# Sliding-window attention into a gated FFN on one core: the attention's second product turned round

## The chip, the cores and the metric

The kernel runs on one core of one Trainium2 chip, in a single launch. The metric is device time in microseconds (us). Before the change three runs took 256.97, 258.34 and 258.73 us, a median of 258.34.

## What is computed

Eight batches of eight heads, 576 positions, head dimension 64. Each position attends to itself and the 63 positions before it; the attention output, heads side by side, is the input of an FFN whose two first products are multiplied element by element.

```python
scores = scale * np.matmul(q, k.transpose(0, 1, 3, 2))
rel = pos[:, None] - pos[None, :]
mask = (rel >= 0) & (rel < window)          # window = 64
attn = softmax(np.where(mask, scores, -1e9))
x = np.matmul(attn, v)                      # 4608 rows of 512 after the heads are put side by side
h = (x @ w1) * (x @ w2) @ w3
out = h @ w_out
```

## The kernel before, in words

All matmul inputs are fp16, and sums are fp32. At the start w3 and w_out are multiplied into one 1024x512 matrix `wc_sb` (`fold_t`, `fold_mm`), so that the FFN's second half is one product.

The attention works in 18 stages of 256 rows (four groups of 64 queries, all eight heads). A stage has these steps:

- `scores(s)` (L265): 64 small matmuls give the scores transposed, 128 keys by 64 queries, in two PSUM tiles `a_ps`. The pool `ps_a` has two such buffers, and scores and values take them in turn, so either step waits until the other's results have been read.
- `weigh(d)` (L281), twice a stage: one exponential on ScalarE (ACT) over 128x1024 writes `pt` in fp16, and the band mask is applied, on VectorE (DVE) by a product with `band`, or on GpSimd (POOL) by the two affine selects of `select`. There is no maximum: a constant shift is used.
- `values(s)` (L295): V is the stationary operand and `pt` moves. Per half of the heads, four matmuls with 32 columns of ones (L301) give each query's sum in 32 rows, and 32 matmuls (L307) give the weighted V, already transposed as the FFN needs it (head dimension on the partitions, queries along the row).
- `norm(s)` (L311): ACT takes Ln of the sums and Exp of minus that, which gives the reciprocals `r`; DVE multiplies both halves by them into `xT` (L320), a ring of 2048 rows.
- `keep_sums(s)` (L324) sends the logarithms by a DMA of the SP queue to `lnsum`. `check_sums` (L451) tests them near the end; if any is out of bounds a general path, which is not taken here, runs behind the fast one.

The FFN works in nine groups of 512 rows. `ffn_ab(g, fc)` (L355) makes eight matmuls of 512 columns, an ACT copy and a DVE product; there are eight of these in a group. `ffn_o(g, t)` (L374), four in a group, makes eight matmuls and one copy out of PSUM, on DVE or ACT. The pool `ps_f` has four buffers, two for each `ffn_ab`.

Inputs arrive by DMAs of the POOL queue. q and k are transposed in 32x32 blocks on DVE (`transposes`, L214). `RUN` says how many rows of q or k lie next to each other in a load: nine for the first three batches, two after that. The transposed words are written with a step of that many words. `copy_v` (L232) copies V rows by half a block, on DVE.

The order of the work is written out by hand (`manual_schedule`): each engine works through its own list in the order in which the program calls the steps. Up to stage 5 every call stands in the program by itself (L479 to L642). From then on a loop takes an FFN slot, then the attention's steps that are due (`tick`, L336): each stage has six units, scores and the first `weigh` at unit 0, the second at unit 1, `values` and `norm` of the stage before at unit 3, `keep_sums` at unit 5. `events` (L328) sets at which unit, counted from a batch's first, its loads, transposes and copies of V are issued.

Of the kernel before, what the change touches and what calls it, by code (L numbers as in the profile page):

```python
# [15 lines left out]
P = 128  # L16
# [123 lines left out]
def kernel(  # L140
# [25 lines left out]
    NU = 6 * NS + 6  # L166
    AHEAD = 18
    START = 42

# [54 lines left out]
    def load_v(b, *blocks):  # L224

        vh = v16s[b % 3]
        for c in blocks:
            lo = D if c == 7 else 0
            s0 = 64 * c + lo
            nc.gpsimd.dma_start(out=vh[lo:P, c], in_=v[b, :, s0:s0 + P - lo, :].rearrange("h s d -> s h d"))  # L230

    def copy_v(b, half, i0, i1):  # L232

        vh = v16s[b % 3].rearrange("p (i o) h d -> p i o (h d)", o=2)
        if half == 0:
            dve_cp(vh[0:D, i0:i1, 1], vh[D:P, i0:i1, 0])
        else:
            dve_cp(vh[D:P, i0:i1, 1], vh[0:D, i0 + 1:i1 + 1, 0])
# [13 lines left out]
    def make_band():  # L252

        nc.gpsimd.memset(band, 1.0)
        select(band)
        nc.gpsimd.memset(band[:, 4], 1.0)
        nc.gpsimd.affine_select(out=band[:, 4], in_=band[:, 4], pattern=[[1, 64]], compare_op=ALU.is_ge,
                                fill=0.0, base=0, channel_multiplier=-1)
# [22 lines left out]
    def weigh(d, engine=nc.gpsimd):  # L281

        pt = probs[d] = sb.tile([P, 4, W], FP16, name="pt", bufs=6)
        nc.scalar.activation(pt, held.pop(d).rearrange("k j (a n) -> k (j a) n", a=2), AF.Exp, bias=-SHIFT, scale=scale)  # L284
        first = [i for i, (b, t) in enumerate(groups(d // 2)) if t == 0]
# [9 lines left out]
    def values(s):  # L295

        o_ps = opened[s] = [ps_a.tile([P, 2, 512], FP32, name="a_ps") for _ in range(2)]
        for jp in range(2):
            pt = probs.pop(2 * s + jp)
            for h in range(4):  # L300
                nc.tensor.matmul(o_ps[0][32 * h:32 * h + 32, 1, W * jp:W * jp + W], ones32, pt[:, h],  # L301
                                 start=True, stop=True, skip_group_check=True)
            for i, (b, t) in enumerate(groups(s)):
                for x in range(2):
                    for h in range(4):
                        o0 = W * x + 64 * i
                        nc.tensor.matmul(o_ps[jp][32 * h:32 * h + 32, 0, o0:o0 + 64],  # L307
                                         v16s[b % 3][:, max(0, t - 1), 4 * jp + h, x:D:2], pt[:, h, 64 * i:64 * i + 64],
                                         start=True, stop=True, skip_group_check=True)

    def norm(s):  # L311

        o_ps = opened.pop(s)
        y = lns[s] = sb.tile([P, 2, W], FP32, name="ln_s", bufs=3)
        r = sb.tile([P, 2, W], FP32, name="r")
        x0 = s * W % RING
        nc.scalar.activation(y, o_ps[0][:, 1].rearrange("p (j n) -> p j n", j=2), AF.Ln)  # L317
        nc.scalar.activation(r, y, AF.Exp, scale=-1.0)  # L318
        for jp in range(2):
            nc.vector.tensor_tensor(xT[:, 2 * jp:2 * jp + 2, x0:x0 + W],  # L320
                                    o_ps[jp][:, 0].rearrange("p (x n) -> p x n", x=2),
                                    r[:, jp].unsqueeze(1).broadcast_to([P, 2, W]), ALU.mult)

    def keep_sums(s):  # L324
        nc.sync.dma_start(out=lnsum[4 * s:4 * s + 4, :], in_=lns.pop(s)[0:P:32].rearrange("a j n -> a (j n)"))
# [120 lines left out]

    rows = 4 * NS
    okv = const.tile([rows, 1], FP32)
    ones = const.tile([rows, 1], FP32)

    def check_sums():  # L451

        chk = const.tile([rows, 2 * W], FP32)
        nc.gpsimd.memset(ones, 1.0)
        nc.gpsimd.tensor_tensor(chk, lnsum, lnsum, ALU.mult)
        nc.gpsimd.tensor_single_scalar(chk, chk, BOUND * BOUND, op=ALU.is_le)
        nc.vector.tensor_reduce(okv, chk, axis=mybir.AxisListType.X, op=ALU.min)
        nc.vector.tensor_scalar(okv, okv, -1.0, 1.0, op0=ALU.mult, op1=ALU.add)
# [15 lines left out]
    def make_ones(engine):  # L474
        engine.memset(ones32, 1.0)

# [56 lines left out]
    values(0)  # L533
    norm(0)
    fold_mm(5, 0, DM, dve_cp)
# [5 lines left out]
    values(1)  # L541
    norm(1)
    fold_mm(6, 0, DM, dve_cp)
# [5 lines left out]
    ffn_ab(0, 2)  # L549
    keep_sums(0)  # L550
    ffn_ab(0, 3)
# [22 lines left out]
    load_v(2, 6, 7)  # L574
    keep_sums(1)
    store()
    norm(2)
    transposes(2, 'k', 0)
# [3 lines left out]
    store()  # L582
    norm(3)
    transposes(2, 'k', 1)
# [9 lines left out]
    store()  # L594
    keep_sums(2)
    scores(4)
# [3 lines left out]
    weigh(9, nc.gpsimd)  # L600
    keep_sums(3)
    weigh(8, nc.gpsimd)
# [16 lines left out]
    values(4)  # L619
    norm(4)  # L620
    transposes(3, 'k', 1)
# [5 lines left out]
    store()  # L627
    norm(5)
    keep_sums(4)
    ffn_o(1, 1, act_cp)  # L630
# [8 lines left out]
    load_qk(4, 'k')  # L639
    keep_sums(5)  # L640
    store()
# [14 lines left out]
    for i, (w, due) in enumerate(slots):  # L656
# [9 lines left out]
        while u < NU and u + 1 <= due + 1e-6:  # L666
# [5 lines left out]

    bad = nc.values_load(bad_i[0:1, 0:1], min_val=0, max_val=4 * NS,
                         skip_runtime_bounds_check_because="a count of 72 flags")
    with tc.If(bad > 0, preferred_fallthrough_block=True, label="range"):
# [30 lines left out]
```

## Time and profile before

| | before |
|---|---|
| runs | 256.97, 258.34, 258.73 us |
| profiled execution, first to last instruction (span) | 256.9 us |
| TensorE (PE) clock granted | 0.999 |
| PE busy | 242.7 us (94%) |
| DVE busy | 146.1 us (57%) |
| ACT busy | 117.9 us (46%) |
| POOL busy | 114.2 us (44%) |

The profiled execution has no time of its own beside its span of 256.9 us: that span is 1.4 us under the median of the runs and next to the fastest of them. Matmuls are pipelined, so that busy time counts several in flight at once; the chain of work that ended last, followed back from the last instruction, says what each stretch of PE work costs in the end. In a row of the chain the first number is the start, the second the time, and "x4" the instructions in it. In a row of the timeline the second number is the time from the first start to the last end.

### The profile page before, as it was taken

The page shows a single profiled execution, that of the slowest core. Times are in us where ns is not written, and L with a number is a line of the kernel's source. Part 1 is how long each engine was busy: PE and PEld are TensorE (multiplying, and loading weights), DVE is VectorE, ACT ScalarE, POOL GpSimd, SP SyncE. Part 2 cuts the span into 40 slices and gives each one's busy share as a digit, 9 for nine tenths or more (in the row PEclk, how much of TensorE's full clock was granted, in tenths as well). Part 3 has the DMA queues.
Part 4 walks back from the last instruction along what each step waited for, and adds up shares of the span by engine and source line. Part 5 has one row for each costly group of instructions (what it writes and reads, how often), then busy time and mean ns, then how long its engine had stood idle before and what let it go on. Part 6 is the DMA issues. An engine that isn't in the chain of part 4 may idle for free.

```text
span 256.9 us, 8221 instructions
## 1 busy us (share of the span) xinstructions
PE 242.7 (94%) x3592; PEld 127.1 (49%) x3592; DVE 146.1 (57%) x218; ACT 117.9 (46%) x177; POOL 114.2 (44%) x153
## 2 busy tenths in 40 slices
PE   2959999999999999999999999999999999999990
PEld 2948654454454544445444444544444445444450
DVE  0346956869676546557764774775566345425330
ACT  3033643385565754454526444545465355233310
POOL 7973857759599746890197036003000303003000
PEclk9999999999999999999999999999999999999999
DMA  6999999979997999699089909501300220031022
GB/s 199 196 202 183 205 205 194 168 143 165 193 142 88 191 197 141 99 192 177 2 124 207 118 0 156 105 5 41 126 3 5 82 87 4 0 126 43 4 82 88
DMA packets 75657, 30.09 MB, mean 117 GB/s; under 512 B 62488, under 2 KB 70040, under 8 KB 75616
## 3 DMA queue, kind: packets, MB, share of 16 engines
q0 software_dynamic: 69712, 18.88, 73.6%
q1 hardware_dynamic: 5616, 10.44, 11.1%
q8 instruction: 29, 0.48, 0.8%
q10 hardware_dynamic: 288, 0.20, 0.2%
q14 instruction: 12, 0.10, 0.1%
HBM read 38.80 MB, written 9.44 MB: 188 GB/s over the span
## 4 chain that ended last, share of the span: by engine, by line
PE 90%; DMA 6%; ACT 1%; issue 1%; DVE 0%; POOLq 0%
PE f_ps L367 49%; PE f_ps L383 24%; PE f_ps L444 6%; PE a_ps L275 4%; PE a_ps L307 4%; DMA ab<-in_moe_w_out_dram 4%; PE a_ps L301 2%; DMA q<-in_q_dram 2%; PE f_ps L437 1%; ACT pt L284 1%; DVE w3T L439 0%; DVE t2k L390 0%; ACT t2k L390 0%; PE f_ps L462 0%; POOLq L701 0%
## 5 line engine op out<-in xcount | busy, mean ns | idle before, releaser
L367 PE MATMUL f_ps<-xT,w_sb 128*128 128x512 f16 x576 | 129.4, 379 | 0.0
L367 PEld LDWEIGHTS <-w_sb 128*128 128x128 f16 x576 | 54.7, 98 | 64.3 <-issue 0.4
L371 DVE TENSOR_TENSOR ab<-f_ps,a_sb 128x512 f16<-128x512 f32 x72 | 49.6, 689 | 40.5 <-PE f_ps L367 38.1
L383 PE MATMUL f_ps<-wc_sb,ab 128*128 128x512 f16 (+1 forms) x296 | 65.6, 374 | 0.0
L370 ACT COPY a_sb<-f_ps 128x512 f32<-128x512 f32 x72 | 42.2, 587 | 47.2 <-PE f_ps L367 47.2
L245 POOL TENSOR_SCALAR_AFFINE_SELECT pt<-pt 128x1024 f16<-128x1024 f16 x11 | 12.6, 1143 | 79.7 <-ACT pt L284 79.6
L383 PEld LDWEIGHTS <-ab 128*128 128x128 f16 x296 | 27.9, 98 | 31.0
L284 ACT ACTIVATE pt<-a_ps 128x1024 f16<-128x1024 f32 x36 | 36.2, 1027 | 12.4 <-PE a_ps L275 12.3
L320 DVE TENSOR_TENSOR xT<-a_ps,r 128x512 f16<-128x512 f32 x36 | 23.2, 686 | 23.5 <-ACT r L318 23.4
L230 POOL DMA_DIRECT2D v<-in_v_dram x40 | 33.8, 862 | 2.3 <-DMA w_sb<-in_moe_w_dram 1.2
L386 ACT COPY t2k<-f_ps 128x512 f32<-128x512 f32 (+1 forms) x21 | 12.1, 576 | 43.4 <-PE f_ps L383 43.4
L288 DVE TENSOR_TENSOR pt<-pt,band 128x1024 f16<-128x1024 f16 x25 | 17.3, 696 | 15.4 <-ACT pt L284 15.2
L210 POOL DMA_DIRECT2D k<-in_k_dram x32 | 20.2, 645 | 6.7 <-DMA v<-in_v_dram 3.3
L210 POOL DMA_DIRECT2D q<-in_q_dram x32 | 20.4, 652 | 4.9 <-DMA v<-in_v_dram 1.9
L220 DVE STREAM_TRANSPOSE qT<-q 128x576 int32<-128x576 int32 x16 | 14.7, 930 | 8.2 <-DMA q<-in_q_dram 8.2
L444 PE MATMUL f_ps<-ab,w3T 128*128 128x256 f16 (+1 forms) x96 | 14.8, 308 | 3.4 <-DMA ab<-in_moe_w_out_dram 3.0
L220 DVE STREAM_TRANSPOSE kT<-k 128x576 int32<-128x576 int32 x16 | 14.8, 936 | 1.1 <-DMA k<-in_k_dram 1.1
L307 PE MATMUL a_ps<-pt,v 128*32 128x64 f16 x1152 | 14.2, 193 | 0.3 <-issue 0.3
L317 ACT ACTIVATE ln_s<-a_ps 128x512 f32<-128x512 f32 x18 | 10.7, 597 | 7.6 <-PE a_ps L301 7.4
L386 DVE COPY t2k<-f_ps 128x512 f32<-128x512 f32 x15 | 10.3, 686 | 6.8 <-PE f_ps L383 6.8
L275 PEld LDWEIGHTS <-kT 32*128 32x128 f16 x1152 | 10.4, 92 | 7.3 <-issue 7.2
L307 PEld LDWEIGHTS <-v 128*32 128x32 f16 x1152 | 13.6, 97 | 0.8 <-issue 0.4
(47 smaller groups left out, 129.1 us busy)
## 6 DMA issues: line engine op xcount, KB each, us to landing
out_dram<-t2k SPq DMA_DIRECT2D x35, 256.0 KB, 3.4
q<-in_q_dram POOLq DMA_DIRECT2D x32, 144.0 KB, 6.2
k<-in_k_dram POOLq DMA_DIRECT2D x32, 144.0 KB, 7.1
v<-in_v_dram POOLq DMA_DIRECT2D x32, 128.0 KB, 5.6
w_sb<-in_moe_w_dram POOLq DMA_DIRECT2D x8, 256.0 KB, 9.7
w_sb<-in_moe_w_dram SPq DMA_DIRECT2D x2, 512.0 KB
ab<-in_moe_w_out_dram POOLq DMA_DIRECT2D x2, 512.0 KB, 9.4
xT<-in_moe_w_dram POOLq DMA_DIRECT2D x2, 512.0 KB, 12.2
```

What stands on the lines that cost most here:

```text
L210: nc.gpsimd.dma_start(out=t16_of(b, which)[32 * j:32 * j + 32].rearrange("p hh (i n) -> p (hh i) n", n=r * D), in_=src[b, 2 * j:2 * j + 2] ...
L220: nc.vector.transpose(dst[b][:, hh].rearrange("q t c -> q (t c)").bitcast(I32).rearrange("q (i p r) -> q i r p", p=32, r=r), t16s[which, b ...
L230: nc.gpsimd.dma_start(out=vh[lo:P, c], in_=v[b, :, s0:s0 + P - lo, :].rearrange("h s d -> s h d"))
L284: nc.scalar.activation(pt, held.pop(d).rearrange("k j (a n) -> k (j a) n", a=2), AF.Exp, bias=-SHIFT, scale=scale)
L307: nc.tensor.matmul(o_ps[jp][32 * h:32 * h + 32, 0, o0:o0 + 64], v16s[b % 3][:, max(0, t - 1), 4 * jp + h, x:D:2], pt[:, h, 64 * i:64 * i + ...
L320: nc.vector.tensor_tensor(xT[:, 2 * jp:2 * jp + 2, x0:x0 + W], o_ps[jp][:, 0].rearrange("p (x n) -> p x n", x=2), r[:, jp].unsqueeze(1).br ...
L367: nc.tensor.matmul(d[:, f * n:f * n + n], w[:, dc, (fc + f) * P:(fc + f + 1) * P], xT[:, dc, x0:x0 + n], start=(dc == 0), stop=(dc == 3), ...
L370: act_cp(a_sb[:, 0:nf * n], a_ps[:, 0:nf * n])
L371: nc.vector.tensor_tensor(ab[:, fc:fc + nf, lo:hi], b_ps[:, 0:nf * n].rearrange("p (f n) -> p f n", f=nf), a_sb[:, 0:nf * n].rearrange("p ...
L383: nc.tensor.matmul(o_ps[:, 0:c1 - c0], ab[:, fc, t * P:t * P + P], wc_sb[:, fc, c0:c1], start=(fc == 0), stop=(fc == 7))
L386: cp(o_sb[:, c0:c1], o_ps[:, 0:c1 - c0])
L444: nc.tensor.matmul(o_ps[:, c0:c1], w3Ts[fc][:, ec, :], wo16[:, ec, c0:c1], start=(ec == 0), stop=(ec == 7))
```

## The change

- The stationary operand of the second product is now `pt`: 32 queries at a time, every second one of a group of 64 (`c` is 0 for the even and 1 for the odd queries). V moves, with a 65th column of ones, so that each query's sum comes out as column 64 of its own row. The ones matmuls go. The V tiles have rows of 96 elements per head (`VW`) to hold the ones.
- The exponential reads every second query of the scores, so that `pt` holds the even queries of a group, then the odd ones; the masks have the same order.
- `norm(s, jp)` works on one half of the heads: a DVE reciprocal of 128x8 sums, a DVE product of 128x512 into `xn`, and a DVE 32x32 block transpose of 128x256 words (pairs of fp16) into `xT`. Ln and Exp go. The first half is issued right after `values`, the second one unit later.
- `keep_sums` and its 18 DMAs go; the reciprocals stay in `rs`, and `check_sums` tests them with three operations on POOL of 128x288.
- In the loop all copies of `ffn_o` go to ACT (even t had been on DVE); the transposes and the second `copy_v` are issued at other units.
- In the part written out by hand, `norm(s, 0)` and `norm(s, 1)` stand where `norm(s)` stood.

```diff
-    lnsum = const.tile([4 * NS, 2 * W], FP32)
-    ones32 = const.tile([P, 32], FP16)
-    v16s = [const.tile([P, 8, H, D], FP16, name=f"v16_{i}") for i in range(3)]
+    rs = const.tile([P, NS, 2, 8], FP32)
+    v16s = [const.tile([P, 8, H, VW], FP16, name=f"v16_{i}") for i in range(3)]
...
     def select(rows):
-        pat = [[0, rows.shape[1]], [1, 64]]
+        pat = [[0, rows.shape[1]], [1, 2], [2, 32]]
+        rows = rows.rearrange("p m (c i) -> p m c i", c=2)
...
-        nc.scalar.activation(pt, held.pop(d).rearrange("k j (a n) -> k (j a) n", a=2), AF.Exp, bias=-SHIFT, scale=scale)
+        nc.scalar.activation(pt.rearrange("k h (g c i) -> k (h g) c i", g=4, c=2),
+                             held.pop(d).rearrange("k j (g i c) -> k (j g) c i", c=2, i=32), AF.Exp, bias=-SHIFT, scale=scale)
...
-            for h in range(4):
-                nc.tensor.matmul(o_ps[0][32 * h:32 * h + 32, 1, W * jp:W * jp + W], ones32, pt[:, h],
-                                 start=True, stop=True, skip_group_check=True)
             for i, (b, t) in enumerate(groups(s)):
-                for x in range(2):
+                for c in range(2):
                     for h in range(4):
-                        o0 = W * x + 64 * i
-                        nc.tensor.matmul(o_ps[jp][32 * h:32 * h + 32, 0, o0:o0 + 64],
-                                         v16s[b % 3][:, max(0, t - 1), 4 * jp + h, x:D:2], pt[:, h, 64 * i:64 * i + 64],
+                        n0 = 64 * i + 32 * c
+                        o0 = 256 * (i % 2) + 128 * c
+                        nc.tensor.matmul(o_ps[jp][32 * h:32 * h + 32, i // 2, o0:o0 + D + 1], pt[:, h, n0:n0 + 32],
+                                         v16s[b % 3][:, max(0, t - 1), 4 * jp + h, 0:D + 1],
                                          start=True, stop=True, skip_group_check=True)
...
+    def norm(s, jp):
+        o = opened[s][jp].rearrange("p k (g c n) -> p (k g) c n", g=2, c=2)
         x0 = s * W % RING
-        nc.scalar.activation(y, o_ps[0][:, 1].rearrange("p (j n) -> p j n", j=2), AF.Ln)
-        nc.scalar.activation(r, y, AF.Exp, scale=-1.0)
-        for jp in range(2):
-            nc.vector.tensor_tensor(xT[:, 2 * jp:2 * jp + 2, x0:x0 + W],
-                                    o_ps[jp][:, 0].rearrange("p (x n) -> p x n", x=2),
-                                    r[:, jp].unsqueeze(1).broadcast_to([P, 2, W]), ALU.mult)
+        r = rs[:, s, jp].rearrange("p (g c) -> p g c", c=2)
+        xn = sb.tile([P, 4, D, 2], FP16, name="xn", bufs=4)
+        nc.vector.reciprocal(r, o[:, :, :, D])
+        nc.vector.tensor_tensor(xn.rearrange("p g d c -> p g c d"), o[:, :, :, 0:D],
+                                r.unsqueeze(3).broadcast_to([P, 4, 2, D]), ALU.mult)
+        nc.vector.transpose(
+            xT[:, 2 * jp:2 * jp + 2, x0:x0 + W].bitcast(I32).rearrange("p x (g i) -> p x g i", i=32),
+            xn.rearrange("p g d c -> p (g d c)").bitcast(I32).rearrange("p (g e x) -> p x g e", e=32, x=2))
...
+        k0, k1, q0, q1 = (-10, -7, -5, -4) if b > 4 else (-7, -5, -4, -1)
-                       (-7, (transposes, "k", 0)), (-5, (transposes, "k", 1)), (-4, (transposes, "q", 0)),
-                       (-2, (transposes, "q", 1)), (2, (copy_v, 0, 0, 4)), (4, (copy_v, 1, 0, 3))):
+                       (k0, (transposes, "k", 0)), (k1, (transposes, "k", 1)), (q0, (transposes, "q", 0)),
+                       (q1, (transposes, "q", 1)), (2, (copy_v, 0, 0, 4)), (5, (copy_v, 1, 0, 3))):
...
             values(s - 1)
-            norm(s - 1)
-        if m == 5 and START // 6 <= s <= NS:
-            keep_sums(s - 1)
+            norm(s - 1, 0)
+        if m == 4 and START // 6 <= s <= NS:
+            norm(s - 1, 1)
...
     def make_ones(engine):
-        engine.memset(ones32, 1.0)
+        for vh in v16s:
+            engine.memset(vh[:, :, :, D:D + 2], 1.0)
...
-        part += [lambda g=g, t=t: ffn_o(g, t, act_cp if t % 2 else dve_cp) for t in range(4)]
+        part += [lambda g=g, t=t: ffn_o(g, t, act_cp) for t in range(4)]
```

More of the change, by code (lines that the diff above doesn't have):

```diff
@@ L1 @@
+import math
 from contextlib import ExitStack
@@ L167 @@
     AHEAD = 18
+    VW = 96
     START = 42
@@ L445, in fold_mm @@
         cp(wc_sb[:, fc, c0:c1], o_ps[:, c0:c1])
-    rows = 4 * NS
-    okv = const.tile([rows, 1], FP32)
-    ones = const.tile([rows, 1], FP32)
+    okv = const.tile([P, 1], FP32)
+    ones = const.tile([P, 1], FP32)
     def check_sums():
-        chk = const.tile([rows, 2 * W], FP32)
+        sums = rs.rearrange("p s j n -> p (s j n)")
+        chk = [const.tile([P, 16 * NS], FP32, name=f"chk_{i}") for i in range(2)]
         nc.gpsimd.memset(ones, 1.0)
-        nc.gpsimd.tensor_tensor(chk, lnsum, lnsum, ALU.mult)
-        nc.gpsimd.tensor_single_scalar(chk, chk, BOUND * BOUND, op=ALU.is_le)
-        nc.vector.tensor_reduce(okv, chk, axis=mybir.AxisListType.X, op=ALU.min)
+        nc.gpsimd.tensor_single_scalar(chk[0], sums, math.exp(-BOUND), op=ALU.is_ge)
+        nc.gpsimd.tensor_single_scalar(chk[1], sums, math.exp(BOUND), op=ALU.is_le)
+        nc.gpsimd.tensor_tensor(chk[0], chk[0], chk[1], ALU.mult)
+        nc.vector.tensor_reduce(okv, chk[0], axis=mybir.AxisListType.X, op=ALU.min)
         nc.vector.tensor_scalar(okv, okv, -1.0, 1.0, op0=ALU.mult, op1=ALU.add)
@@ L533 @@
     values(0)
-    norm(0)
+    norm(0, 0)
+    norm(0, 1)
     fold_mm(5, 0, DM, dve_cp)
@@ L541 @@
     values(1)
-    norm(1)
+    norm(1, 0)
+    norm(1, 1)
     fold_mm(6, 0, DM, dve_cp)
@@ L574 @@
     load_v(2, 6, 7)
-    keep_sums(1)
     store()
-    norm(2)
+    norm(2, 0)
+    norm(2, 1)
     transposes(2, 'k', 0)
@@ L582 @@
     store()
-    norm(3)
+    norm(3, 0)
+    norm(3, 1)
     transposes(2, 'k', 1)
@@ L594 @@
     store()
-    keep_sums(2)
     scores(4)
@@ L619 @@
     values(4)
-    norm(4)
+    norm(4, 0)
+    norm(4, 1)
     transposes(3, 'k', 1)
@@ L627 @@
     store()
-    norm(5)
-    keep_sums(4)
+    norm(5, 0)
+    norm(5, 1)
     ffn_o(1, 1, act_cp)
@@ L671 @@
     fast.close()
-    bad = nc.values_load(bad_i[0:1, 0:1], min_val=0, max_val=4 * NS,
-                         skip_runtime_bounds_check_because="a count of 72 flags")
+    bad = nc.values_load(bad_i[0:1, 0:1], min_val=0, max_val=P,
+                         skip_runtime_bounds_check_because="a count of 128 flags")
     with tc.If(bad > 0, preferred_fallthrough_block=True, label="range"):
```

20 lines of the change are left out of this document (6 added, 14 removed).

## The prediction

> **What bounds the kernel now.** I read the page first: its span, the busy times, and the chain of work that ended last.
>
> ```profile
> span 256.9 us, 8221 instructions
> ...
> PE 242.7 (94%) x3592; PEld 127.1 (49%) x3592; DVE 146.1 (57%) x218; ACT 117.9 (46%) x177; POOL 114.2 (44%) x153
> ...
> PE 90%; DMA 6%; ACT 1%; issue 1%; DVE 0%; POOLq 0%
> ```
>
> TensorE (PE) is 90% of the chain. ScalarE (ACT) and VectorE (DVE) are almost absent from it, so work taken off ACT is worth nothing by itself, and work given to DVE costs nothing until DVE makes PE wait. Next, the same chain in order of time, one values step of the loop:
>
> ```profile
> 106.35 0.22 PE a_ps L301 x4
> 106.58 0.24 PE a_ps L307 x32
> 106.82 0.11 PE a_ps L301 x4
> 106.93 0.24 PE a_ps L307 x32
> 107.18 3.56 PE f_ps L383 x16
> 110.73 1.73 PE f_ps L367 x8
> ```
>
> The step takes 107.18 - 106.35 = 0.83 us. The second four ones matmuls take 0.11, the first four 0.22: the other 0.11 is paid at the entry from the wide matmuls, whoever comes first. One FFN slot of eight matmuls is 1.73, so one wide matmul is 0.216. Then the groups by line, which price what goes and what comes:
>
> ```profile
> L284 ACT ACTIVATE pt<-a_ps 128x1024 f16<-128x1024 f32 x36 | 36.2, 1027 | 12.4 <-PE a_ps L275 12.3
> ...
> L320 DVE TENSOR_TENSOR xT<-a_ps,r 128x512 f16<-128x512 f32 x36 | 23.2, 686 | 23.5 <-ACT r L318 23.4
> ...
> L318 ACT ACTIVATE r<-ln_s 128x512 f32<-128x512 f32 x18 | 11.3, 630 | 0.6
> L317 ACT ACTIVATE ln_s<-a_ps 128x512 f32<-128x512 f32 x18 | 10.7, 597 | 7.6 <-PE a_ps L301 7.4
> ...
> L463 DVE CAST bad_i<-f_ps 1x1 int32<-1x1 f32 x1 | 0.1, 136 | 0.0
> ```
>
> Last, DVE's load by stretch, since an average of 57% hides where it is full (the columns are PE, PEld, DVE, ACT, POOL):
>
> ```profile
> 24.00:38.00 14.00, 14.00 (x293) 8.71 (x291) 10.91 (x19) 7.41 (x10) 9.37 (x14) 1.00 1.32 202
> ...
> 50.00:66.00 16.00, 15.91 (x329) 7.89 (x328) 13.24 (x18) 9.70 (x15) 12.16 (x15) 1.00 1.17 166
> ...
> 90.00:114.00 24.00, 23.67 (x367) 11.60 (x366) 13.22 (x20) 11.50 (x18) 17.57 (x23) 1.00 1.40 152
> ```
>
> DVE is 10.91 of 14 us busy around stages 0 and 1, and 13.24 of 16 around stages 2 and 3, against 13.22 of 24 in the loop. The prediction turns on the first two.
>
> **The change, part by part.** PE first. Without the ones matmuls a values step is 0.11 (entry) + 0.24 + 0.24 = about 0.60, with 1/64 of the 0.48 more for the 65th column. Weights stay 128x32, and 32 matmuls follow each other as before. Saving 0.22 a stage, 18 x 0.22 = 4.0 us if nothing else happens.
>
> ACT loses 18 x (0.60 + 0.63) = 22 us and gains 14 `ffn_o` copies; it is not on the path. The exponential of 1.03 us now reads every second element; no row shows that. I take it as unchanged and put its price under the rivals.
>
> DVE loses two products a stage and gains two halves of `norm`. Two rows price an instruction that waits for the one before it on DVE, and two the block transposes:
>
> ```profile
> 58.69 1.22 DVE L220 STREAM_TRANSPOSE kT<-k 128x576 int32<-128x576 int32 x1
> ...
> 73.90 0.78 DVE L220 STREAM_TRANSPOSE qT<-q 128x576 int32<-128x576 int32 x1
> ...
> 79.65 1.43 DVE L220 STREAM_TRANSPOSE kT<-k 128x576 int32<-128x576 int32 x2
> ```
> ```profile
> 234.97 0.68 DVE L457 TENSOR_REDUCE okv<-chk 72x1 f32<-72x512 f32 x1 [0.59 <-POOL chk L456]
> 235.69 0.15 DVE L458 TENSOR_SCALAR okv<-okv 72x1 f32<-72x1 f32 x1
> ```
>
> The second instruction reads the first's result and starts 235.69 - 234.97 - 0.68 = 0.04 after its end. Independent ones start before the last has ended: two transposes take 1.43, so the second starts 1.43 - 0.78 = 0.65 after the first, 0.13 before its end. The new transpose has 256 words, not 576: in proportion 0.29, with a fixed part of 0.1 to 0.15 about 0.33 until the next may start (estimate from these rows). The reciprocal of eight numbers out of PSUM I put at 0.16, just above the 0.136 of the one-element cast. So one half of `norm` holds DVE for 0.16 + 0.04 + 0.69 + 0.04 + 0.33 = 1.26 us. From below 1.2 (0.14 and 0.29); from above 1.6, if the transpose pays for its stepped reading what the transpose at 58.69 pays for writing with a step of nine words where the others have two (1.22 against 0.78 for 576 words: 0.76 ns a word, 0.2 in all) and the reciprocal twice its price. I take 1.26, as a step of two words is what the 0.78 row has.
>
> The Trainium skill, "VectorE: DVE Perf Modes", section "Walkthrough: the 8-slice pipeline in each mode", says that the reciprocal runs its divide with a repeat count of eight. At its 0.96 GHz that would be an estimated 0.07 for eight numbers instead of 0.01, a half of 1.32 and a sum 0.6 us higher; no run here shows it.
>
> Now PE, ACT and DVE are followed through the part written by hand, in the clock of before. **Stages 0 and 1:**
>
> ```profile
> 30.90 1.29 DVE L320 TENSOR_TENSOR xT<-a_ps,r 128x512 f16<-128x512 f32 x2
> 32.11 0.68 DVE L445 CAST wc_sb<-f_ps 128x512 f16<-128x512 f32 x1
> 32.80 0.29 DVE L236 COPY v<-v 64x512 f16<-64x512 f16 x1
> 33.01 0.68 DVE L439 COPY w3T<-f_ps 128x1024 f16<-128x1024 f16 x1
> ```
> ```profile
> 28.67 0.22 PE a_ps L301 x4
> ...
> 31.32 0.89 PE f_ps L437 x16
> ...
> 33.04 3.56 PE f_ps L444 x16
> 36.60 13.81 PE f_ps L367 x64
> ```
>
> DVE gets to `norm(0)` at 30.90 both before and after, since work queued ahead of it ends then. After: first product done 31.79, second at 30.90 + 1.26 + 0.16 + 0.04 + 0.69 = 33.05, DVE free at 33.42. `values(1)` could start at 32.0 (31.32 + 0.89 less 0.22), but its second half needs the buffer that the second product frees: 33.10, so it ends at 33.35 and the two `fold_mm` behind it at 36.91. DVE goes on with the cast (0.69), the copy (0.21) and w3T (0.61): `norm(1)` starts at 34.93 and ends, last transpose in full, at 37.56. The first `ffn_ab` starts at 36.91, has two matmuls' worth of `xT`, waits until 37.61 and ends at 37.61 + 6 x 0.216 = 38.91. Before: 36.60 + 1.73 = 38.33. **+0.58.**
>
> **Stages 2 and 3:**
>
> ```profile
> 56.50 0.68 DVE L386 COPY t2k<-f_ps 128x512 f32<-128x512 f32 x1
> ```
> ```profile
> 56.40 1.83 PE f_ps L383 x8
> ...
> 59.24 1.83 PE f_ps L383 x8
> 61.08 0.47 PE f_ps L367 x2
> ...
> 61.55 4.91 PE f_ps L367 x22
> ```
>
> Before, `ffn_ab(1, 0)` started at 61.08, did the two matmuls that the first product had made ready, and went on at 61.55: nothing was to spare. After: DVE starts `norm(2)` at 57.11 (56.50 + 0.68, less 0.07 of overlap), as it no longer waits for Ln and Exp, and frees the buffers at 58.00 and 59.26. PE ends `ffn_o(0, 2)` at 58.01, `values(3)` gets its second buffer at 59.31 and ends at 59.56, `ffn_o(0, 3)` at 61.39. On DVE the k transpose (1.22 - 0.13 = 1.09 until the next) stands behind `norm(2)` from 59.63, so `norm(3)` starts at 60.72 and ends at 63.35. `ffn_ab(1, 0)` then does its last six matmuls from 63.40, ending at 64.70, against 61.55 + 1.30 = 62.85. **+1.85.** The two transposes and the product behind it are as late as before relative to PE, so no more is lost.
>
> **Stages 4 and 5:** two values steps save 0.44; the second waits 0.1 for `norm(4)`. **-0.35.** **Stages 6 to 17:** `norm` starts about 0.45 after the step's start and ends 2 x 1.26 + 0.1 later, at 3.1; the first wide matmul that needs it comes 0.60 + 3.56 = 4.16 after that start. Slack 1.1, and no DVE copy stands between, since the copies moved to ACT; the moved transposes stand at units with an FFN slot ahead of the step. 12 x 0.22: **-2.64.**
>
> At nothing: `keep_sums` (SP, nobody on the path waits), `check_sums` (three POOL operations, idle POOL, DVE reads them a slot later), the longer selects (POOL waits for ACT most of the time), memsets at the start (DVE waits for q), `copy_v` (runs of 64 stay together; were it paid like the product, 0.69 for 512 elements, the 2048 and 1536 elements copied ahead of stage 2 would take 4.8 us, some 2 of them beyond the slack).
>
> Sum: 0.58 + 1.85 - 0.35 - 2.64 = -0.56, say -0.6. Against the execution's span, 256.9 to 256.3; it stands 1.4 below the runs' median, so in that measure 258.34 - 0.6 = **257.7**. Each 0.1 us more in a half of `norm` delays the first two stretches by four halves each: about 0.8, and with stages 4 and 5 about 1 us.
>
> **The rivals.** *The gain stays:* 18 x 0.22 off, 254.4. For it speaks that DVE idles 43%; against, that 61.08 and 61.55 leave no slack and one product alone, 0.69, is longer than the 0.6 that a half had. *DVE as the bound:* a strided fp16 write slows the product, or the transpose is dear. At the 0.76 ns a word above the product would be 1.08; already at a half of 1.6 the sum is -0.6 + 3.4: 261.1, slower by 1%; that is where it decides. *The exponential pays for its step:* 1024 x 0.76 ns, 1.8 us instead of 1.03. The waits of stage 2 and 3 for two pairs of them grow by 1.6 each and the start by 0.8: +4, 261.7. The loop would hide it, with three slots between scores and values. *PE does not gain:* loads of `pt` are not hidden and each four matmuls take 60 ns, not 30: 288 x 0.03 = 8.6 more, 266. Same shapes speak against it.
>
> The Trainium skill, "PSUM — Partial Sum Buffer", section "Specifications (TRN2)", says that PSUM has lines of 8 bytes and that any access that isn't contiguous slows matmuls significantly; it says that of matmuls, and no run here shows whether ScalarE's reads are meant. By it the exponential's rival would hold.
>
> **How the numbers follow.** Forecast 0.55, gain stays 0.15, DVE as the bound 0.15, exponential 0.10, PE 0.05. About 1%, 2.6 us, is what a measurement tells from no change. The first is within 1% (its own range 257.1 to 259.5, for halves of 1.2 to 1.44); the second is faster; the others slower, but for 0.03 of a milder exponential. Faster 0.15, same 0.58, slower 0.27. The range runs from the second, 254.4, to just short of the exponential in full, 261.6; PE's rival and the dearer half of DVE's stay out.
>
> **What would show it.** Values steps of 0.6 in the chain; exponentials of 1.03; halves of 1.26 on DVE; waits of PE for DVE at `values(1)`, `values(3)` and at the first `ffn_ab` of groups 0 and 1, about 3 us in all, and none in the loop. Wrong if DVE's halves are longer or the loop's first `ffn_ab` waits as well.

## The result, and the profile after

| | before | after |
|---|---|---|
| runs | 256.97 to 258.74 us (4) | 284.09 to 286.28 us (4) |
| median | 258.53 us | 284.70 us |
| after / before | | 1.103 (95%: 1.099 to 1.108) |
| profiled execution: time | none of its own | 284.09 us |
| profiled execution: span | 256.9 us | 282.4 us |

The kernel became slower by 26 us, where 0.6 us less was forecast. A run's time stands 1.7 to 1.9 us above its span in the runs listed here (284.09 against 282.4), so the span of 256.9 of before belongs to a run of about 258.6 us, near the median, and not to the fastest. The page of after, the same three lines as were shown of before:

```profile
span 282.4 us, 7897 instructions
...
PE 242.2 (86%) x3448; PEld 124.5 (44%) x3448; DVE 161.0 (57%) x278; ACT 104.2 (37%) x155; POOL 118.5 (42%) x154
...
PE 66%; DVE 16%; DMA 7%; issue 3%; ACT 3%; POOL 2%; DVEq 0%; POOLq 0%; ACTq 0%
```

PE is busy as long as before (242.2 us against 242.7) in a span that is 25.5 us longer, and DVE has 16% of the chain of work that ended last, where it had 0%. So PE is not busy for longer; it waits for DVE. The view of waits of after says where (in total, how often, the longest):

```profile
PE f_ps L367 <- DVE xT L322: 20.4, 14, 2.0
...
PEld L367 <- DVE xT L322: 3.8, 2, 2.1
...
PEld L437 <- DVE xT L322: 3.3, 1, 3.3
...
PE f_ps L437 <- DVE xT L322: 2.8, 1, 2.8
```

L322 is the new transpose, L367 the wide matmuls of `ffn_ab`, L437 a step of the fold of w3 (`fold_t`). The wide matmuls wait fourteen times, 1.5 us on average, where the prediction had two such waits, at the first slots of groups 0 and 1. Twelve of them, 19.1 us, lie in the loop, two in each of groups 2 to 7. To place them, take four marks of the chain in order of time: the first matmul of group 0 (36.60 before), the last six of `ffn_ab(1, 0)` (61.55), the first of group 2, and the last run of `ffn_o`. Of before:

```profile
86.21 1.73 PE f_ps L367 x8
...
244.17 6.94 PE f_ps L383 x40
```

And of after, with a part of the loop between:

```profile
39.88 13.81 PE f_ps L367 x64
...
67.06 4.91 PE f_ps L367 x22
...
91.76 1.73 PE f_ps L367 x8
...
101.36 0.74 DVE xn L320
102.12 0.46 DVE xT L322
102.62 1.69 PE f_ps L367 x7
104.40 0.69 DVE ab L371
105.09 0.13 DVE rs L319
105.24 0.74 DVE xn L320
106.00 0.46 DVE xT L322
106.50 2.97 PE f_ps L367 x13
...
115.37 0.64 PE a_ps L309 x62
116.00 3.56 PE f_ps L383 x16
119.56 1.73 PE f_ps L367 x8
...
129.28 0.46 DVE xT L322
129.78 1.92 PE f_ps L367 x8
...
133.39 0.46 DVE xT L322
133.89 3.18 PE f_ps L367 x14
...
268.80 6.94 PE f_ps L383 x40
```

After lags by 3.28 at the first mark, 5.51 at the second, 5.55 at the third and 24.63 at the fourth. The loop from group 2 on lasted 157.96 us before and 177.04 after: 19.1 us are lost there, and 0.9 more in the tail behind the fourth mark (12.73 before, 13.60 after). In that loop PE is idle for 19.9 us (177.04 less 157.10 busy), and was idle for 0.3 before. In the chain both halves of an even stage's `norm` stand in PE's way, each followed by the matmuls of an FFN slot less one (x7) or less three (x13 is five and a whole slot); in groups 3 and 7 by a whole slot (x8) or a slot less two (x14 is six and a whole slot). Each half stands on DVE behind the `ab` product of an FFN slot just done (the rows from 104.40 on), and so comes late for the next slot. An odd stage (115.37) costs nothing: `ffn_o`, which does not read `xT`, follows it for 3.56 us.

The matmuls done ahead of the wait, one or three in most groups, are the clue. In the loop a stage writes the columns of `xT` for the *next* group; the slots that wait belong to the *current* one and read other columns. The list of waits in the built program says which matmuls of `ffn_ab` wait for a write of `norm`, past the first matmul of a group (`dc` is the row of `xT` that a matmul reads, `fc` the slot):

```
before          every group but 2           fc 0: dc 2
after           groups 2, 4, 5, 6           fc 0: dc 2    fc 4: dc 1    fc 5: dc 3
after           groups 3, 7 (ring wraps)    fc 0: dc 2    fc 4: dc 0    fc 5: dc 2
```

A transpose writes two stretches, the same 256 columns in rows 2jp and 2jp+1 of the 4x2048 tile. If a wait is derived for everything from the first to the last word written, half 0 at column x0 covers the rest of row 0 and all of row 1 up to x0+256: the current group's columns, left of x0, are in it for `dc` 1. Half 1 hits `dc` 3 in the same way. Where the ring wraps, x0 is 0 and the current group lies at columns 1536 to 2047, inside row 0 and row 2: `dc` 0 and `dc` 2. These are the pairs of the list. The same reading gives the wait at L437: half 1 of stage 0 covers all of row 2, where a piece of w3 is parked. The product that wrote `xT` before had the same two stretches and no such wait; it wrote 16-bit elements, the transpose writes 32-bit words through a view of the 16-bit tile. (Group 2 is missing in the line of before, since an earlier matmul there already waits for that product.)

### The profile page after: what moved, and what is told of

Read it like the earlier page. It is cut to its first block, busy times and chain, and to the rows that moved or that the text cites. A ratio compares the mean times of both kernels' runs of the same rounds, so it can differ in the third digit from the quotient of the medians.

```text
span 282.4 us, 7897 instructions
## 1 busy us (share of the span) xinstructions
PE 242.2 (86%) x3448; PEld 124.5 (44%) x3448; DVE 161.0 (57%) x278; ACT 104.2 (37%) x155; POOL 118.5 (42%) x154
## 4 chain that ended last, share of the span: by engine, by line
PE 66%; DVE 16%; DMA 7%; issue 3%; ACT 3%; POOL 2%; DVEq 0%; POOLq 0%; ACTq 0%
PE f_ps L367 40%; PE f_ps L383 17%; DVE xn L320 5%; PE f_ps L444 4%; PE a_ps L278 4%; DVE ab L371 3%; DMA ab<-in_moe_w_out_dram 3%; DVE xT L322 3%; DMA k<-in_k_dram 2%; ACT pt L287 2%; DMA q<-in_q_dram 2%; PE a_ps L309 2%; POOL v L231 1%; PE f_ps L437 1%; DVE rs L319 1%
## 5 line engine op out<-in xcount | busy, mean ns | idle before, releaser
L367 PE MATMUL f_ps<-xT,w_sb 128*128 128x512 f16 x576 | 131.2, 379 | 21.3 <-DVE xT L322 20.4
L367 PEld LDWEIGHTS <-w_sb 128*128 128x128 f16 x576 | 54.6, 98 | 87.7 <-issue 21.4
L247 POOL TENSOR_SCALAR_AFFINE_SELECT pt<-pt 128x1024 f16<-128x1024 f16 x11 | 14.3, 1302 | 96.8 <-ACT pt L287 96.8
L287 ACT ACTIVATE pt<-a_ps 128x1024 f16<-128x1024 f32 x36 | 36.2, 1026 | 12.4 <-PE a_ps L278 12.3
L386 ACT COPY t2k<-f_ps 128x512 f32<-128x512 f32 (+1 forms) x35 | 20.3, 580 | 48.9 <-PE f_ps L383 48.9
L320 DVE TENSOR_TENSOR xn<-a_ps,rs 128x512 f16<-128x512 f32 x36 | 26.2, 729 | 1.2
L292 DVE TENSOR_TENSOR pt<-pt,band 128x1024 f16<-128x1024 f16 x25 | 17.4, 701 | 12.8 <-ACT pt L287 12.5
L211 POOL DMA_DIRECT2D q<-in_q_dram x32 | 20.4, 649 | 8.0 <-DMA v<-in_v_dram 4.0
L322 DVE STREAM_TRANSPOSE xT<-xn 128x256 int32<-128x256 int32 x36 | 16.0, 445 | 1.2
L249 POOL TENSOR_SCALAR_AFFINE_SELECT pt<-pt 128x1024 f16<-128x1024 f16 x11 | 14.6, 1331 | 0.8
L309 PEld LDWEIGHTS <-pt 128*32 128x32 f16 x1152 | 10.6, 95 | 9.1 <-issue 6.8
L309 PE MATMUL a_ps<-v,pt 128*32 128x65 f16 x1152 | 13.0, 195 | 1.6 <-DVE xn L320 1.3
L319 DVE RECIPROCAL rs<-a_ps 128x8 f32<-128x8 f32 x36 | 6.7, 186 | 13.1 <-PE a_ps L309 13.1
```

The lines of the kernel that those rows point to most:

```text
L211: nc.gpsimd.dma_start(out=t16_of(b, which)[32 * j:32 * j + 32].rearrange("p hh (i n) -> p (hh i) n", n=r * D), in_=src[b, 2 * j:2 * j + 2] ...
L287: nc.scalar.activation(pt.rearrange("k h (g c i) -> k (h g) c i", g=4, c=2), held.pop(d).rearrange("k j (g i c) -> k (j g) c i", c=2, i=32 ...
L309: nc.tensor.matmul(o_ps[jp][32 * h:32 * h + 32, i // 2, o0:o0 + D + 1], pt[:, h, n0:n0 + 32], v16s[b % 3][:, max(0, t - 1), 4 * jp + h, 0: ...
L320: nc.vector.tensor_tensor(xn.rearrange("p g d c -> p g c d"), o[:, :, :, 0:D], r.unsqueeze(3).broadcast_to([P, 4, 2, D]), ALU.mult)
L322: nc.vector.transpose(xT[:, 2 * jp:2 * jp + 2, x0:x0 + W].bitcast(I32).rearrange("p x (g i) -> p x g i", i=32), xn.rearrange("p g d c -> p ...
L367: nc.tensor.matmul(d[:, f * n:f * n + n], w[:, dc, (fc + f) * P:(fc + f + 1) * P], xT[:, dc, x0:x0 + n], start=(dc == 0), stop=(dc == 3), ...
```

## Experiments

The theory: **a false wait.** The framework that builds the program derives, for a write of 32-bit words in two stretches into the 16-bit tile, a wait that spans both; the loss is that wait. The rivals: **DVE is too slow or its order is wrong** (the prediction's own rival, with copies and moved transposes as variants), and **the new instructions themselves cost PE time**.

**e1, one unbroken stretch a write.** `xT` is laid out by stages, so that the two rows of a transpose lie side by side. The pieces of w3 that are parked in `xT` move to the slots of stages 4 to 7; all else stays.

```diff
-    xT = const.tile([P, NJ, RING], FP16)
+    xT = const.tile([P, RING // W, NJ, W], FP16)
...
-            xT[:, 2 * jp:2 * jp + 2, x0:x0 + W].bitcast(I32).rearrange("p x (g i) -> p x g i", i=32),
+            xT[:, x0 // W, 2 * jp:2 * jp + 2, :].bitcast(I32).rearrange("p x (g i) -> p x g i", i=32),
...
-                                     xT[:, dc, x0:x0 + n], start=(dc == 0), stop=(dc == 3), skip_group_check=True)
+                                     xT[:, x0 // W:(x0 + n) // W, dc, :], start=(dc == 0), stop=(dc == 3), skip_group_check=True)
```

> The changed kernel with the ring xT laid out by stages: 8 slots of 4x256 instead of 4 rows of 2048, so that each transpose writes one unbroken stretch; nothing else differs. Theory W (wide wait): the transpose writes 32-bit words into a 16-bit tile in two stretches, and the wait that the framework derives covers everything from the first to the last word, so that TensorE waits for a norm whose rows it does not read. Then the waits of L367 for the transpose (20.4 us) fall below 3 us, the fold's wait (2.8 us) goes, and the span falls from 282.4 to about 259 (257 to 262). Theory D (VectorE is the bound: the longer halves of norm, 1.35 us, are late by themselves): the order on VectorE and its work are the same, so the span stays above 276.

Measured: 261.17 us median (260.54 to 263.31), 1.010 of before (1.007 to 1.014), in the range expected. The group of the wide matmuls in e1 (busy, mean ns, idle before them and what ended it):

```profile
L367 PE MATMUL f_ps<-xT,w_sb 128*128 128x512 f16 x576 | 129.6, 379 | 2.2 <-DVE xT L322 1.3 <-ACT a_sb L370 0.9
```

The waits for the transpose fall from 20.4 to 1.3 us, with the same instructions on DVE in the same order. In the chain of e1 a stage of the loop runs without DVE:

```profile
124.13 0.64 PE a_ps L309 x61
124.76 5.29 PE f_ps L367 x24
130.05 0.61 PE a_ps L278 x56
130.66 1.83 PE f_ps L367 x8
```

Its loop, by the same two marks, lasts 248.05 - 91.82 = 156.23 us, 1.7 less than before. What remains, 2.8 us at the medians, is ahead of the loop and in the tail. The profiled execution of e1 is the slowest of its five runs (263.31 us): its first fold matmuls took 1.3 us longer at a lower granted clock (the last section has the numbers).

**e2, the old layout, two transposes a half.** Each writes one row: twice the instructions, each in one stretch.

```diff
-        nc.vector.transpose(
-            xT[:, 2 * jp:2 * jp + 2, x0:x0 + W].bitcast(I32).rearrange("p x (g i) -> p x g i", i=32),
-            xn.rearrange("p g d c -> p (g d c)").bitcast(I32).rearrange("p (g e x) -> p x g e", e=32, x=2))
+        for x in range(2):
+            nc.vector.transpose(
+                xT[:, 2 * jp + x, x0:x0 + W].bitcast(I32).rearrange("p (g i) -> p g i", i=32),
+                xn.rearrange("p g d c -> p (g d c)").bitcast(I32).rearrange("p (g e x) -> p x g e", e=32, x=2)[:, x])
```

> The changed kernel with its old layout of xT, but each half's transpose split in two, one for each row of xT, so that each writes one stretch; VectorE has 36 more instructions and some 36 x 0.17 = 6 us more work. Theory W: the loop's waits go as with the new layout, and the span is 259 to 263, the longer halves costing 0.5 to 2 us in the part written by hand. Theory D: with more work on VectorE the span rises above 283. Should it be the layout's reading or writing that matters, this one, which keeps it, stays near 282.

Measured: 263.24 us in one run, span 261.5; the waits of the wide matmuls for the transpose are 1.3 us, the loop lasts 156.06. So it is the two stretches in one write that matter, not the layout, and 36 more instructions on DVE cost next to nothing there.

**e3 and e4, the wait without the change.** The kernel before, with its products written to a small tile and copied into `xT`: as 32-bit words in e3, as 16-bit elements in e4. No transpose, no turned matmul.

```diff
-            nc.vector.tensor_tensor(xT[:, 2 * jp:2 * jp + 2, x0:x0 + W],
+            xn = sb.tile([P, 2, W], FP16, name="xn", bufs=4)
+            nc.vector.tensor_tensor(xn,
                                     o_ps[jp][:, 0].rearrange("p (x n) -> p x n", x=2),
                                     r[:, jp].unsqueeze(1).broadcast_to([P, 2, W]), ALU.mult)
+            dve_cp(xT[:, 2 * jp:2 * jp + 2, x0:x0 + W].bitcast(I32), xn.bitcast(I32))   # e3
+            dve_cp(xT[:, 2 * jp:2 * jp + 2, x0:x0 + W], xn)                             # e4
```

> The kernel before the change, its second product as it was, but norm's two VectorE products go to a small tile, and from there by a VectorE copy of 32-bit words into xT. Theory W: TensorE waits in seven even stages for both copies, about 1.9 us each time, so 10 to 16 us more than the same kernel with 16-bit copies (next run). Theory D: no difference between the two beyond 2 us.

> As the run before, but the copies are of 16-bit elements; the same bytes. Both theories: the kernel before plus the delay of 36 copies in the part written by hand, 0 to 4 us: 257 to 262 in the span, with no wait of L367 for xT in the even stages of the loop.

Measured: e3 282.21 us, e4 258.74 us, in one run each, beside 258.40 for the kernel before on that chip. The wide matmuls of e3:

```profile
L369 PE MATMUL f_ps<-xT,w_sb 128*128 128x512 f16 x576 | 135.8, 389 | 13.4 <-DVE xT L324 13.3
```

and of e4:

```profile
L369 PE MATMUL f_ps<-xT,w_sb 128*128 128x512 f16 x576 | 129.4, 379 | 0.8 <-DVE xT L324 0.8
```

The two kernels move the same bytes with the same number of instructions, and a copy into `xT` takes 295 ns (median) in both; only the element size of one view differs, and e3 takes 23.5 us longer. That settles the kind of cause: a wait that the program contains, not a slow instruction. The list of waits agrees: e4, like e1 and e2, has none at `fc` 4 or 5; e3 has `dc` 1 and `dc` 3 (where the ring wraps, `dc` 0 and `dc` 2), both at `fc` 4, since its two copies are issued one behind the other.

Not all of the 23.5 us are waits. By the marks e3's loop lasts 267.52 - 90.36 = 177.16 us and e4's 157.57, 19.6 less. PE is idle in e3's loop for 13.0 us, 12.5 of them in waits for the copy, at one place in each of groups 2 to 7, and in e4's not at all; that is within the 10 to 16 us expected. The other 6.6 us are PE work that took longer (164.15 us busy in e3's loop, 157.57 in e4's). A lower granted clock goes with it: the clock's row shows lower slices in e3 alone (each digit is a fortieth of the span, in tenths of full speed), and from 100 to 110 us and from 150 to 160 us the clock was 0.83. The pages of e3 and e4:

```profile
PE 250.5 (89%) x3592; PEld 128.9 (46%) x3592; DVE 158.9 (57%) x254; ACT 118.1 (42%) x177; POOL 114.2 (41%) x153
...
PEclk9999999999999979999999799999999999899998
```
```profile
PE 244.6 (95%) x3592; PEld 128.2 (50%) x3592; DVE 158.3 (62%) x254; ACT 117.9 (46%) x177; POOL 113.6 (44%) x153
...
PEclk9999999999999999999999999999999999999999
```

So it is chance that e3's loop is as long as that of after (177.04), where PE idles for 19.9 us at a clock of 1.00. Whether the waits bring the clock down no run shows.

**e5, less DVE work in the part written by hand.** e1, with five copies and casts of stages 0 to 3 moved from DVE to ACT, `copy_v(0, 0, 3, 4)` behind `norm(1)`, and the k transpose from between `norm(2)` and `norm(3)` to behind `norm(3)`.

```diff
-    fold_mm(4, 0, DM, dve_cp)
+    fold_mm(4, 0, DM, act_cp)
...
     norm(2, 0)
     norm(2, 1)
-    transposes(2, 'k', 0)
...
     norm(3, 0)
     norm(3, 1)
+    transposes(2, 'k', 0)
```

> The layout by stages of e1, and VectorE relieved in the part written by hand: the casts of fold 4, 5 and 6, the copy behind fold_t(7) and that of ffn_o(0, 1) go to ScalarE, one copy of V stands behind norm(1), and the first transpose of batch 2's k behind norm(3) instead of ahead of it. Theory H (what is left of e1's excess over the kernel before is VectorE's longer halves in the hand-written stages 0 to 3): the waits of values(1), values(3) and of the first ffn_ab of groups 0 and 1, some 3.5 us in e1, fall to 1 us, and the median falls by 2 to 3.5 us from e1's 261.2, to 257.7 to 259.2. Theory S (the excess is in the start, where w_out's load lands later, or in the loop): within 1 us of e1.

Measured: 259.79 us (258.19 to 260.71, 12 runs), 1.0045 of before (1.0022 to 1.0067). Better than e1 by some 1.4 us, less than the 2 to 3.5 expected. The timeline of e5 shows one reason:

```profile
31.20 0.43 PE L309 MATMUL a_ps<-v,pt 128*32 128x65 f16 x32 [1.24 <-ACT pt L287]
```

The cast of `fold_mm(4)` now stands on ACT ahead of an exponential that `values(0)` waits for: work moved off one in-order queue delayed another.

**e6 and e7, the moved copies and events of the change undone**, each on e1: even `ffn_o` copies back on DVE; transposes and `copy_v` at the units of before.

```diff
-        part += [lambda g=g, t=t: ffn_o(g, t, act_cp) for t in range(4)]
+        part += [lambda g=g, t=t: ffn_o(g, t, act_cp if t % 2 else dve_cp) for t in range(4)]   # e6
...
-        k0, k1, q0, q1 = (-10, -7, -5, -4) if b > 4 else (-7, -5, -4, -1)
+        k0, k1, q0, q1 = (-7, -5, -4, -2)                                                       # e7
```

> e1 with the copies of ffn_o at even t back on VectorE in the loop, as before the change. The prediction put this edit at nothing. If that holds: within 1 us of e1 (260.2 to 262.2). If the norm of the odd stages needs VectorE free of copies: a wait of up to 0.6 us in each of seven groups, up to 4 us more.

> e1 with the transposes and the second copy of V at the units of before (-7, -5, -4, -2 and 4). The prediction put this edit at nothing: within 1 us of e1. If it matters, a transpose at unit 4 or a copy between the two halves of norm holds the second half back by 0.7 us in five batches, at most 3 us more.

Measured: e6 261.96 us (261.43 to 263.63), 1.013 (1.009 to 1.017); e7 261.78 us (260.25 to 262.79), 1.012 (1.007 to 1.017). Both within 1 us of e1's 261.17 with overlapping intervals: neither part of the change moves the time by an amount that these runs can tell.

**e8, the halves of a `norm` step by step.** e5 with the cast of `fold_mm(4)` back on DVE; up to stage 5, both reciprocals are issued first, then both products, then both transposes.

```diff
-    def norm(s, jp):
+    def norm(s, *jps):
...
+        for jp in jps:
...
+            nc.vector.reciprocal(r[jp], os[jp][:, :, :, D])
+        for jp in jps:
+            nc.vector.tensor_tensor(xn[jp].rearrange("p g d c -> p g c d"), os[jp][:, :, :, 0:D],
+                                    r[jp].unsqueeze(3).broadcast_to([P, 4, 2, D]), ALU.mult)
+        for jp in jps:
+            nc.vector.transpose(
...
-    norm(2, 0)
-    norm(2, 1)
+    norm(2, 0, 1)
```

> e5, but the cast of fold 4 stays on VectorE (in e5 it stood ahead of an exponential that values(0) waits for), and in stages 0 to 5 the two halves of norm are issued step by step: both reciprocals, both products, both transposes, so that no step waits for the one just ahead of it and the second buffer comes free one transpose earlier. Theory H (the excess over the kernel before is VectorE's work in the hand-written stages): the second half's product ends some 0.5 us earlier and a whole norm takes 2.4 us, not 2.7; the median falls by 1 to 2 us from e5's 259.8, to 257.8 to 258.8, level with the kernel before. Theory S (start and end of the program): within 0.7 us of e5.

Measured: 256.90 us (256.24 to 258.29, 12 runs), 0.9956 of before (0.9942 to 0.9971). It beats both kernels, and lies below the 257.8 to 258.8 expected. Its wide matmuls:

```profile
L371 PE MATMUL f_ps<-xT,w_sb 128*128 128x512 f16 x576 | 129.3, 380 | 0.2 <-DVE xT L326 0.2
```

Stage 2 in the timeline of after, one half behind the other:

```profile
60.54 0.19 DVE L319 RECIPROCAL rs<-a_ps 128x8 f32<-128x8 f32 x1
60.76 0.73 DVE L320 TENSOR_TENSOR xn<-a_ps,rs 128x512 f16<-128x512 f32 x1
...
61.52 0.45 DVE L322 STREAM_TRANSPOSE xT<-xn 128x256 int32<-128x256 int32 x1
...
61.89 0.17 DVE L319 RECIPROCAL rs<-a_ps 128x8 f32<-128x8 f32 x1
...
62.86 0.45 DVE L322 STREAM_TRANSPOSE xT<-xn 128x256 int32<-128x256 int32 x1
```

and in that of e8, step by step:

```profile
56.83 0.27 DVE L321 RECIPROCAL rs<-a_ps 128x8 f32<-128x8 f32 x2
57.06 1.36 DVE L323 TENSOR_TENSOR xn<-a_ps,rs 128x512 f16<-128x512 f32 x2
...
58.30 0.76 DVE L326 STREAM_TRANSPOSE xT<-xn 128x256 int32<-128x256 int32 x2
```

In after a half holds DVE for 61.89 - 60.54 = 1.35 us, and each of its steps waits for the one before. In e8 both halves are through in 58.30 + 0.76 - 56.83 = 2.23 us instead of 62.86 + 0.45 - 60.54 = 2.77, and the second `a_ps` buffer is free sooner, as both products now stand ahead of the transposes. The marks of e8's chain:

```profile
36.78 13.81 PE f_ps L371 x64
...
85.86 1.73 PE f_ps L371 x8
...
241.06 6.94 PE f_ps L387 x40
```

Group 2 starts 0.35 us ahead of before (e1: 5.61 behind, of which 2.1 had arisen by the fold's 40 matmuls, in part through the clock), and the loop lasts 155.20 us, 2.76 less than before.

**e9, e10, e11, is e8's gain only a better order?** e9 and e10 move `make_band()` behind a later load of w3, in e8 and in the kernel before; e11 gives the kernel before the moved copies, casts and transpose of e5.

```diff
-    make_band()
...
     load_w3(4, 2)
+    make_band()
```

> e8 with make_band issued behind the first loads of w3 and w_out on the POOL queue instead of ahead of them. The selects of the changed kernel are longer (0.74 for 0.66 us on 128x512), and the loads behind them start later. If that delays the fold: 0.5 to 2 us off, and the same edit on the kernel before (next run) brings nearly as much. If the loads wait for the DMA engines anyway: within 0.5 us of e8.

> The kernel before the change with the same move of make_band: the control for e9, so that its gain is not put down to the change. If the fold waits for loads behind make_band: 0.5 to 2 us under the kernel before (256.3 to 257.8). If not: within 0.5 us of it.

> The control for e8: the kernel before the change with the same copies and casts moved from VectorE to ScalarE in the hand-written part and the first transpose of batch 2's k behind norm(3). If e8's gain is that of the turned product, this stays within 0.7 us of the kernel before, as ScalarE still has Ln and Exp there. If e8's gain is only that of a better order, this falls by 1 us or more as well.

Measured: e9 256.34 us (255.81 to 259.63), 0.9946 (0.9923 to 0.9970); e10 258.29 us, 0.9996 (0.9982 to 1.0011); e11 258.32 us, 1.0010 (0.9982 to 1.0038). The band's place does nothing that can be told in either kernel, and the relief of DVE gives the kernel before nothing that can be told. So e8's gain, 0.44% or 1.1 us, does not come from these moves, which the kernel before could have had as well. The layout by stages, the moved `ffn_o` copies and the moved events were not tried in the kernel before; e6 and e7 give no sign that the last two are worth as much, and the wide matmuls of before had no waits for a layout to remove (0.0 idle). What is left as the source is the turned product with its `norm` step by step.

**e12, e8 in the old layout.** `xT` and its readers as in the kernel after, all else as in e8.

```diff
-    xT = const.tile([P, RING // W, NJ, W], FP16)
+    xT = const.tile([P, NJ, RING], FP16)
```

> e8 with the layout of xT of the changed kernel. Theory W: the waits of the loop are back, 20 us of L367 for the transpose, and the span is 274 to 280. If e8's edits had cured the waits in another way: under 262.

Measured: 282.04 us in one run, span 280.3, just above the 274 to 280 expected. Its wide matmuls:

```profile
L371 PE MATMUL f_ps<-xT,w_sb 128*128 128x512 f16 x576 | 132.5, 383 | 18.8 <-DVE xT L326 18.8
```

Its loop lasts 266.86 - 89.62 = 177.24 us, as in after. The layout is all that e12 and e8 differ in, and it separates 282.04 us from 256.90, so the order of the halves does not help against the false wait.

## Why the prediction was wrong

The lags at the marks split the 25.5 us of the two spans: 3.28 up to the first FFN slot, 2.23 in stages 2 and 3, 0.04 in stages 4 and 5, 19.08 in the loop, 0.87 behind it.

- **The step that failed: "Stages 6 to 17".** It took "the first wide matmul that needs it" as the first that may wait, and found a slack of 1.1 us. The loop's matmuls of the current group need nothing that `norm` writes at that time, but the program makes them wait: +19.1 instead of -2.64. The nearest of its signs, "the loop's first `ffn_ab` waits as well", names the first slot of a group, where the waits came at the fifth and sixth, and no rival with a price stood behind it. The prediction costed a new write by its duration alone and not by the waits that follow from how it writes. e1 shows that the loop gains 1.7 us once these waits are gone, and e3 that they come without the turned product.
- **Stages 0 and 1: "+0.58".** Measured +3.28 in this execution: w_out's load let the fold start 0.60 later (16.65 us against 16.05; over the profiled executions of all kernels, with and without the change, it starts between 15.0 and 16.9), and `fold_t` waits 2.8 us for the same false reason. The walk along the queues had L437 start when PE got there. Without the false wait, in e1 and e8, the stretch counted from the fold's 40 matmuls (19.91 before, 22.02 in e1, 19.61 in e8) costs 1.2 and 0.5.
- **Stages 2 and 3: "+1.85".** Measured +2.23, through the waits that were forecast: `values(3)` for its second buffer, `norm(3)` behind the k transpose, the last six matmuls of `ffn_ab(1, 0)`. Mechanism right, size 0.4 low; four halves of `norm`, each 0.09 too cheap (next point), are about as much.
- **A half of `norm`: "1.26 us".** Measured 1.35: 0.22 from the reciprocal to the product, 0.76 to the transpose, 0.37 to the next half; expected were 0.20, 0.73 and 0.33. The groups of after, by line:

```profile
L287 ACT ACTIVATE pt<-a_ps 128x1024 f16<-128x1024 f32 x36 | 36.2, 1026 | 12.4 <-PE a_ps L278 12.3
...
L320 DVE TENSOR_TENSOR xn<-a_ps,rs 128x512 f16<-128x512 f32 x36 | 26.2, 729 | 1.2
...
L322 DVE STREAM_TRANSPOSE xT<-xn 128x256 int32<-128x256 int32 x36 | 16.0, 445 | 1.2
...
L319 DVE RECIPROCAL rs<-a_ps 128x8 f32<-128x8 f32 x36 | 6.7, 186 | 13.1 <-PE a_ps L309 13.1
```

  The strided product costs 43 ns more than the old one, the reciprocal of eight numbers 186 ns where 160 were put. The Trainium skill, "VectorE: DVE Perf Modes", section "Walkthrough: the 8-slice pipeline in each mode", has the divide repeat eight times, which the prediction turned into an estimate of 0.06 us more a half; the measured reciprocal is 0.03 above the value put, so it lies between the two. The prediction's own rule, about 1 us for each 0.1 in a half, gives 0.9 for the 0.09: with that the change without the false wait would have stood at about +0.3, where e1 measured +2.8 and e8, which shortens a pair of halves to 2.23, -1.3 (by the medians). In e1's trace every term comes out higher than forecast: +1.2 (without the later start of the fold), +2.3, 0.0, -1.7, and 0.8 in the tail, which was put at nothing; together +2.6.
- **Stages 4 and 5: "-0.35".** Measured 0.04: no gain. The second half of `values(5)` waits 0.45 us for `norm(4)`'s second product (until 85.32 in the timeline of after), where 0.1 was put; a transpose of q and an `ab` product stand ahead of `norm(4)` on DVE.
- **The values step: "about 0.60".** It is 0.64 (115.37 and 124.13 in the chains above), so the turned matmuls save 0.19 a stage and not 0.22. PE does gain, which refutes that rival: where nothing waits (e8), the loop is 2.76 us shorter, against 2.64 forecast. That the two are so close is partly luck: twelve steps at 0.19 give 2.3, and 0.33 of the rest is a wait of the kernel before (at 94.59 in its chain) that e8 does not have.
- **The exponential "unchanged": right.** 1026 ns against 1027, though it reads every second element. The Trainium skill's rule on accesses that aren't contiguous ("PSUM — Partial Sum Buffer", "Specifications (TRN2)") does not show in ScalarE's reads of this kernel; the rule speaks of matmuls.
- **"At nothing".** Right, as far as the runs can tell, for the moved `ffn_o` copies and events (e6, e7), and for `copy_v` in the loop (690 ns for 64x2048 in both kernels). Not quite right for the selects: they take 1302 and 1331 ns instead of 1143 and 1171, and weight loads of `values` wait for them for 1.3 us in after and e1 and 0.8 in e8, in two places each, where none did before.
- **"DVE as the bound".** Its price for a half, 1.6 or more, was not reached; DVE is busy for 57% of the span in both kernels. That DVE's share of the chain went from 0% to 16% is no sign of load: the wait decides when its result is asked for.

What stays open: the tail behind the last matmuls is 0.7 to 0.9 us longer in every kernel with the change than in the one before, also in e8, and no run took it apart. One wait of PE for ACT (0.9 us, the row of e1) stands at 96 us in after and e7 too, and neither in before nor in e8; the copy it waits for stands on ACT behind an exponential (from 94.16 in after), but no run took it apart. How the framework tracks a write was read from the waits, not from its code.

## What to carry to other kernels

A changed instruction is costed twice: by its duration, and by the waits that follow from the shape of what it writes. Where a tile is written through a view of another element size, or in several stretches, look at which readers the program makes wait, and lay the tile out so that each write is one unbroken stretch; here that took 23.5 of the 26 us back (e1). Chains of dependent steps on one in-order engine overlap when their steps are issued in turn; here a pair of halves took 2.23 us instead of 2.77.

## What the runs showed of the hardware beside

- A pair of dependent DVE chains (reciprocal, product, transpose) takes 2.23 us issued step by step and 2.77 us one after the other, since independent neighbours overlap: two transposes of 128x256 words take 0.76 us together and 0.45 alone.
- Two transposes of 128x128 words (e2) take 291 ns each, one of 128x256 takes 445 ns: the fixed part by these two points is about 0.14 us, and a word of a row 1.2 ns.
- An affine select on POOL over the same 128x1024 elements takes 14% longer (1302 against 1143 ns) with one more dimension in its pattern.
- The fold's first 16 matmuls took 1.91 us in the profiled executions of before and after, at a granted clock of 1.00, and 3.17 in e1's, at 0.58 (16.85 to 20.06 us). e2 and e6 show the same, with 3.38 and 3.29 us. What lowers the clock there the runs do not say; it alone moves a single execution by 1.3 us.
